# Polysketch attention followed by hashed experts: an early token class of two batches, groups of 256 and 320 slots, and the last weights loaded beside attention

## The chip, the cores and the metric

The kernel runs on one core of a Trainium2 chip. The time is the device time of one execution in microseconds (us); lower is better. The profile is of one execution of the same program and spans from its first to its last instruction, so its span (203.0 us) is a little shorter than the measured time. PE is the matrix engine, DVE the vector engine, ACT the scalar engine, POOL the general engine and SP the engine that only issues transfers.

## The reference

Two stages are chained. The first is a linear attention: queries and keys of 4 batches, 4 heads, 1088 positions and 32 dimensions are mapped to 64 features, which are the outer product of two sketches of 8 numbers.

```
phi(x) = outer(S1 x, S2 x)                    # 8 x 8 = 64 features
kv = sum_s phi(k)[s] v[s];  z = sum_s phi(k)[s]
attn = (phi(q) kv) / (phi(q) z + 1e-6)        # per batch and head
x = attn as rows: 4 * 1088 = 4352 tokens of 4 * 32 = 128 columns
expert of a token = (token_id * 2654435761) % 8
out = relu(x w1[expert]) w2[expert]           # w1 128 x 1024, w2 1024 x 128
```

Everything is in float32. A token is (batch, position), so the first two batches are tokens 0 to 2175. The expert of a token depends on its id alone and not on the attention, so the routing can be worked out while the attention still runs.

## The kernel before, in words

The kernel is one function with the order of every engine written out by hand: each engine executes its instructions in program order, and an instruction waits for the data or the buffer that it needs. In the text, b is the third batch (index 2) and e the fourth (index 3), the last two.

**Attention.** For each batch, keys are transposed on PE, multiplied with the sketches (L383), copied by ACT, and turned into features by DVE (L411). `kv_products` (L442) accumulates kv and z. `kv_diagonal` (L465) spreads the result into a block-diagonal matrix m, and `kv_tail` does so for the last 64 positions. `q_features` makes the query features and transposes them in blocks (fT, L495). `x_products` (L547) multiplies fT with m and ACT copies the product to xe; `x_tail_products` (L557) does the tail. These products use the two PSUM buffers of the pool `ps_x` in turn. `denominators` (L570, L571) and `x_main` (L576) divide, into the single buffer `xs`, and SP stores the rows to the DRAM tensor `x_rows` (L584); `x_tail` (L590, L592) stores the tail. Batch b's rows are stored in two halves, one for each group of query blocks.

**Routing.** Tokens of an expert are counted and ranked on DVE and PE while the first batches run. Each expert has two classes of slots, early and late, of `GN` = 288 slots each. A token may take an early slot only if its row belongs to the first `EP` partitions of the token table; EP covers the first two batches and the first half of the third (2686 tokens). `route_end` writes the tables `get` (row to gather for each slot) and `put` (row to scatter to). There are 16 groups: early slots of experts 0 to 7, then late slots of experts 0 to 7. Should an expert have more tokens than slots, a loop at the end takes the rest in turns.

**Experts.** Slots are handled in chunks of three tiles of 128 slots (`CT` = 3, 12 chunks, while a group is 2.25 tiles). `fetch_tile` (L674) gathers 128 rows by an indirect DMA that POOL issues; `paced` first copies the indices on DVE (L712), so that the gather's place in time is tied to DVE's work. The chunk becomes columns in one of two ways: `bring` transposes it on PE (L722) and evicts it, or `turn_in` splits it into 16-bit halves on DVE (L729), SP transposes them by DMA (L730) and `join_in` puts them together (L734). Before, chunks 0 to 2 are brought and chunks 3 to 11 are turned in.

Group g has eight slots in time; slot c holds `layer1(g, c)` (L789, two matmul instructions) and `layer2(g-1, c)` (L796). ACT and DVE take turns to evict layer1's product with the relu (L680, L682), from four PSUM buffers. Other work is hung on the slots by `at(g, c, ...)`: gathers, chunks, the transposes of results (`turn_out`, `join_out`, L843 and L851) and the scatters to the output (L799).

**Loads.** SP loads the weights of experts 0 to 3 after the inputs, of 4 and 5 after the rows of batch 0 are stored, and of 6 and 7 behind the rows of batch e (L134, L135; 0.5 MB each).

Of the kernel before, what the change touches and what calls it, by code (L numbers as in the profile page):

```python
# [30 lines left out]
def kernel(  # L31
# [31 lines left out]
    GN = 288  # L63
    EB = B - 2
    EP = (EB * S + SM // 2) // C
    NE = EP * C
    HT = E * GN // P
    ST = 2 * HT
    OT = -(-(N - GN) // P)
    WARM = 10  # L70
    assert E * GN % P == 0 and GN >= P and ST <= P
# [42 lines left out]
    def parts(b, tag="q"):  # L114


        return 2 if b == 0 or b == EB and tag == "q" else 1
# [14 lines left out]
    def load_experts(es):  # L132
        for e in es:
            nc.sync.dma_start(w1[:, e], moe_w1[e])  # L134
            nc.sync.dma_start(w2[:, e], moe_w2[e].rearrange("(c p) d -> p c d", p=P))  # L135
# [155 lines left out]
    def route_ranks(cnt):  # L291
        nc.vector.tensor_scalar(took[:], cnt[:, 2], float(GN), None, op0=OP.min)
        nc.vector.tensor_tensor(left[:], cnt[:, 1], took[:], op=OP.subtract)
        nc.vector.tensor_tensor(seq[:], seq[:], cnt[:, 0].unsqueeze(2).to_broadcast([P, E, C]), op=OP.add)
        nc.vector.tensor_mul(seq[:], seq[:], mask[:])
        nc.vector.tensor_reduce(rank[:], seq[:].rearrange("p e c -> p c e"), axis=AX.X, op=OP.add)

    def route_slots():
        nc.vector.tensor_tensor(both[:], mask[:], took[:].unsqueeze(2).to_broadcast([P, E, C]), op=OP.mult)
        took_t = const.tile([P, C], F32, name="took_t")  # L300
        nc.vector.tensor_reduce(took_t[:], both[:].rearrange("p e c -> p c e"), axis=AX.X, op=OP.add)

        late = const.tile([P, C], F32, name="late")
        nc.vector.memset(late[:], 1.0)
        nc.vector.tensor_scalar(late[0:EP], rank[0:EP], float(GN), None, op0=OP.is_gt)
        nc.vector.tensor_tensor(pos[:], rank[:], took_t[:], op=OP.subtract)
        nc.vector.tensor_mul(pos[:], pos[:], late[:])
        slot = const.tile([P, C], F32, name="slot")
        nc.vector.tensor_scalar(slot[:], took_t[:], -1.0, float(E * GN), op0=OP.mult, op1=OP.add)
        nc.vector.tensor_mul(slot[:], slot[:], late[:])  # L310
        nc.vector.tensor_add(slot[:], slot[:], rank[:])
        nc.vector.scalar_tensor_tensor(slot[:], eid[:], float(GN), slot[:], op0=OP.mult, op1=OP.add)
        over = const.tile([P, C], F32, name="over")
        nc.vector.tensor_scalar(over[:], pos[:], float(GN), float(2 * ST * P), op0=OP.is_gt, op1=OP.mult)
        nc.vector.scalar_tensor_tensor(slot[:], slot[:], -1.0, over[:], op0=OP.add, op1=OP.add)
        slot_i = const.tile([P, C], I32, name="slot_i")
        nc.vector.tensor_copy(slot_i[:], slot[:])
        st_i = const.tile([P, 2, C], I32, name="st_i")
        nc.vector.tensor_scalar(st_i[:, 0], slot_i[:], P.bit_length() - 1, None, op0=OP.logical_shift_right)
        nc.vector.tensor_scalar(st_i[:, 1], slot_i[:], P - 1, None, op0=OP.bitwise_and)  # L320
        nc.vector.tensor_copy(st[:].rearrange("p k c x -> p (k c) x"),
                              st_i[:].rearrange("p k c -> p (k c)").unsqueeze(2).to_broadcast([P, 2 * C, 2]))
# [364 lines left out]
    BG, BT = 4, 4 * GN // P  # L687
    assert BG * GN == BT * P and ST % BT == 0
    xTs = {}

    def x_columns(lo, hi):
        b = lo // (BT * P)
        if b not in xTs:
            xTs[b] = rows_in.tile([P, BT * P], F32, tag="xT", name="xT", bufs=2)
        return xTs[b][:, lo - b * BT * P:hi - b * BT * P]
# [3 lines left out]
    CT = 3  # L699
    xg3, turned_in = {}, {}  # L700

    def fetch_tile(i, at_once=False):
        k, j = divmod(i, CT)
        if j == 0:
            xg3[k] = rows_in.tile([P, CT, DM], F32, tag="xg3", name="xg3", bufs=3)
        gather(xg3[k][:, j], get[:, i:i + 1] if at_once else paced(get[:, i:i + 1]), NE if i < HT else N)

    def paced(idx):


        t = moe.tile([P, 1], I32, tag="idx", name="idx", bufs=4)
        nc.vector.tensor_copy(t[:], idx)  # L712
        return t[:]

    def fetch(k):
        for j in range(CT):
            fetch_tile(k * CT + j, True)

    def bring(k):
        xp = ps_x.tile([P, CT, P], F32, tag="x", name="xp")  # L720
        for j in range(CT):
            nc.tensor.transpose(xp[:, j], xg3[k][:, j], ident[:])  # L722
        evict(k, x_columns(k * CT * P, (k + 1) * CT * P), xp[:].rearrange("p a b -> p (a b)"))

    def turn_in(k):
        xh = moe.tile([P, 2, CT * DM], U16, tag="xh", name="xh", bufs=2)
        turned_in[k] = moe.tile([P, 2, CT, P], U16, tag="xh_turned", name="xh_turned", bufs=2)
        for x in range(2):
            nc.vector.tensor_copy(xh[:, x], _half(xg3[k][:].rearrange("p a b -> p (a b)"), x))  # L729
        nc.sync.dma_start_transpose(turned_in[k][:].rearrange("p x a b -> p (x a) b"), xh[:].rearrange("p x b -> p (x b)"))  # L730

    def join_in(k):
        for x in range(2):
            nc.vector.tensor_copy(_half(x_columns(k * CT * P, (k + 1) * CT * P), x),  # L734
                                  turned_in[k][:, x].rearrange("p a b -> p (a b)"))
# [12 lines left out]
    route_end(idx)  # L748
    kp = k_features(abk, T, work, "")
    x_products(b, 0, fTs[0], m)  # L750
    denominators(b, 0, HQ)
    x_main(b, 0, nc.vector)
    fetch(0)
    kv = kv_products(e, (kp, va), (kp_tail, va_tail))
    fT = q_features(abq, 0)
    last_m = kv_diagonal(e, kv)
# [3 lines left out]
    fetch(1)  # L760
    fTs = [fT, q_features(abq, 1)]
    denominators(b, HQ, GQ * HQ + H)
    x_main(b, 1, nc.vector)
    x_tail(b, nc.vector)
    for g in range(GQ):
        x_products(e, g, fTs[g], last_m)
    bring(0)
    x_tail_products(e, m_tail)
# [4 lines left out]
    load_experts(range(E - 2, E))  # L773
# [8 lines left out]
    G = 2 * E  # L782
    hTs, ops = {}, {}

    def layer1(g, c, lo=0, hi=GN):
        if c == 0 and lo == 0:
            hTs[g] = moe.tile([P, FC, GN], F32, tag="hT", name="hT", bufs=2)
        hp = bank([P, GN], "hp")
        nc.tensor.matmul(hp[:, 0:hi - lo], w1[:, g % E, c * P:(c + 1) * P], x_columns(g * GN + lo, g * GN + hi),  # L789
                         start=True, stop=True)  # L790
        evict(c, hTs[g][:, c, lo:hi], hp[:, 0:hi - lo], relu=True)

    def layer2(g, c, lo=0, hi=GN):
        if c == 0:
            ops[g] = ps_o.tile([P, GN], F32, tag="o", name="op")
# [18 lines left out]
    TURN = (G - 3) * GN // P  # L814
# [4 lines left out]
    def half_columns(x, lo, hi):  # L819
        b = lo // (BT * P)  # L820
        if (b, x) not in halves:
            halves[b, x] = moe.tile([P, BT * P], U16, tag=f"half{x}", name=f"half{x}", bufs=2)
        return halves[b, x][:, lo - b * BT * P:hi - b * BT * P]

    def out_columns(g, lo=0, hi=GN):

        mid = min(max(LATE - g * GN, lo), hi)
        if mid > lo:
            for x in range(2):
                nc.scalar.copy(half_columns(x, g * GN + lo, g * GN + mid), _half(ops[g][:, 0:mid - lo], x))  # L830
        if hi > mid:
            nc.scalar.copy(late_cols[:, g * GN + mid - LATE:g * GN + hi - LATE], ops[g][:, mid - lo:hi - lo])
# [41 lines left out]
    def overflow_tables():  # L874
        nc.vector.tensor_scalar(nt[:], left[:], float(P - 1 - GN), 0.0, op0=OP.add, op1=OP.max)
# [19 lines left out]
        nc.vector.tensor_scalar(begin[:], begin[:], float(P), float(GN), op0=OP.mult, op1=OP.add)  # L895
# [11 lines left out]
    at(1, 6, bring, 2)  # L907
    for j, n in enumerate((1, 4, 7)):
        at(*slot(n), fetch_tile, 2 * CT + j)
    for k in range(3, ST // CT):  # L910
        for j in range(CT):
            at(*slot((k * CT * P // GN - 1) * FC - 19 + 7 * j // 2), fetch_tile, k * CT + j)
    for k in range(3, ST // CT):
        first = k * CT * P // GN
        at(first - 1, 0, turn_in, k)
        at(first - 1, 5, join_in, k)
    for g in range(2, G - 1):
        at(g, 1, turn_out, (g - 1) * GN // P)
        at(g, 5, join_out)
        for c in (6, 7):  # L920
            at(g, c, scatter_next)
        at(g + 1, 3, scatter_next)
        if g in (G - 5, G - 2):

# [16 lines left out]

    g, lo = G - 1, GN - P
    mid = g * GN // P
    for c in range(FC):
        layer2(g - 1, c)
        if c == 2:
            scatter_next()
            out_rows(TURN, 2)
# [3 lines left out]
    for c in range(FC):  # L952
        layer1(g, c, 0, lo)
        if c == 3:
            out_rows(TURN + 2, mid - TURN - 2)
# [5 lines left out]
    for c in range(FC):  # L961
        layer1(g, c, lo, GN)
# [4 lines left out]
    assert not ready and mid == TURN + 4 == ST - 3  # L967
    op = ps_o.tile([P, DM], F32, tag="o", name="op_rows")
    for c in range(FC):
        nc.tensor.matmul(op[:], hTs[g][:, c, lo:GN], w2[:, g % E, c], start=(c == 0), stop=(c == FC - 1))  # L970
# [11 lines left out]
    with tc.For_i(0, turns):  # L982
# [37 lines left out]
        xg = rows_in.tile([P, CT, DM], F32, tag="xg3", name="xg3", bufs=3)  # L1020
# [52 lines left out]
```

## Time and profile before

| | |
|---|---|
| time, median of 3 | 204.04 us (203.92 to 204.78) |
| span of the profile | 203.0 us |
| PE busy | 191.7 us (94%) |
| DVE, ACT, POOL busy | 109.1, 75.0, 93.8 us |
| layer1 and layer2 of full width (128x288) | 480 matmul instructions, 78.5 and 76.7 us |
| gathers, scatters | 36 and 36, about 1.0 us each on POOL |
| transposes by DMA in and out | 9 and 26 |
| moved by DMA | 25.82 MB |

Matmuls overlap, so their mean length (414 ns for 128x288) is longer than the distance between two of them; for what PE costs, the distance counts. The line named in a wait is that of the instruction which was the last to signal by the profile, and a wait for several signals can be put down to a wrong one. A label such as 128x288 gives partitions and elements of a partition.

### The profile page before, as it was taken

The numbers are of one execution on the slowest core, as the hardware profiler recorded it, in microseconds if no ns is written. First come the engines' busy times: TensorE is split into PE (matmuls) and PEld (weight loads), VectorE is DVE, ScalarE is ACT, GpSimd is POOL, SyncE is SP. The second block draws the span as 40 slices with busy tenths as digits, with TensorE's granted clock in tenths as the row PEclk, the third lists the DMA queues.
The fourth block names the chain that finished last, engine by engine and source line by source line (L and its number), as shares of the span: only waits on it lengthen the run. The fifth ranks groups of instructions, "written<-read, shape, count | busy, mean of one in ns | idle before, by whom it ended". The sixth has DMA issues, their size and how long they took to land. (4 is left out here: it accounts for less than half of the span.)

```text
span 203.0 us, 3360 instructions
## 1 busy us (share of the span) xinstructions
PE 191.7 (94%) x1081; PEld 158.7 (78%) x1081; DVE 109.1 (54%) x290; ACT 75.0 (37%) x228; POOL 93.8 (46%) x113
## 2 busy tenths in 40 slices
PE   8999999999997899899999999999999999999970
PEld 3798999999996576677777777777777777777970
DVE  6699799999785232242542533633435654331330
ACT  6624965746454222322313223223322323311330
POOL 6002202728018875447427687426677503324750
PEclk9999999999999699999999999999999999999997
DMA  5948999998013179214215224124224133110000
GB/s 140 293 105 244 335 358 347 330 374 268 3 55 95 42 253 332 58 26 120 71 34 129 55 65 103 46 71 110 71 61 99 49 78 85 33 50 26 30 35 12
DMA packets 40321, 25.82 MB, mean 127 GB/s; under 512 B 20730, under 2 KB 37371, under 8 KB 40304
## 3 DMA queue, kind: packets, MB, share of 16 engines
q1 hardware_dynamic: 37840, 20.98, 36.3%
q0 software_dynamic: 2304, 4.59, 7.5%
q8 instruction: 9, 0.15, 0.3%
q14 instruction: 8, 0.07, 0.1%
q10 hardware_dynamic: 160, 0.04, 0.1%
HBM read 17.47 MB, written 4.59 MB: 109 GB/s over the span
## 5 line engine op out<-in xcount | busy, mean ns | idle before, releaser
L789 PE MATMUL hp<-xT,w 128*128 128x288 f32 (+2 forms) x272 | 83.2, 400 | 0.2 <-ACT xT L680 0.2
L796 PE MATMUL op<-hT,w 128*128 128x288 f32 (+1 forms) x256 | 79.1, 399 | 0.0
L682 DVE TENSOR_SCALAR hT<-hp 128x288 f32<-128x288 f32 (+2 forms) x68 | 29.9, 439 | 66.3 <-PE hp L789 55.7
L789 PEld LDWEIGHTS hp<-xT,w 128*128 128x128 f32 x272 | 50.8, 194 | 13.4 <-ACT xT L680 0.3
L796 PEld LDWEIGHTS op<-hT,w 128*128 128x128 f32 x256 | 47.7, 190 | 12.5
L680 ACT ACTIVATE hT<-hp 128x288 f32<-128x288 f32 (+2 forms) x68 | 27.3, 401 | 68.9 <-PE hp L789 68.9
L799 POOL DMA_INDIRECT out_dram<-os,put x36 | 36.4, 1010 | 33.3 <-DVE os L851 14.4
L674 POOL DMA_INDIRECT xg<-x_rows,idx x30 | 31.2, 1040 | 26.0 <-DVE idx L712 19.5
L547 PE MATMUL x_ps<-m,fT 128*128 128x132 f32 x128 | 16.3, 281 | 0.5 <-DVE den L570 0.3
L442 PE MATMUL kv<-va,kp 128*128 128x132 f32 x128 | 15.8, 278 | 0.5 <-ACT va L608 0.5
L547 PEld LDWEIGHTS x_ps<-m,fT 128*128 128x128 f32 x128 | 15.0, 190 | 1.2 <-issue 0.5
L442 PEld LDWEIGHTS kv<-va,kp 128*128 128x128 f32 x128 | 14.9, 190 | 1.0 <-issue 1.0
L576 POOL TENSOR_TENSOR xs<-xe,den 128x512 f32<-128x512 f32 x6 | 7.7, 1300 | 17.2 <-DVE den L571 17.2
L830 ACT COPY half<-op 128x288 uint16<-128x288 uint16 (+1 forms) x26 | 9.1, 400 | 13.0 <-PE op L796 13.0
L674 POOL DMA_INDIRECT xg<-x_rows,get x6 | 7.2, 1200 | 11.7 <-DVE m L465 10.1
L465 ACT COPY m<-kv 32x66 f32<-32x66 f32 x48 | 9.9, 207 | 4.2 <-PE kv L442 3.6
L411 DVE TENSOR_TENSOR f<-ab 128x1024 f32<-128x1024 f32 x8 | 10.6, 1321 | 0.4 <-ACT ab L399 0.2
L495 DVE STREAM_TRANSPOSE fT<-f 128x1024 f32<-128x1024 f32 x8 | 10.0, 1245 | 0.5
L411 DVE TENSOR_TENSOR kp<-ab 128x1024 f32<-128x1024 f32 x8 | 9.4, 1206 | 1.0 <-ACT ab L399 1.0
L383 PE MATMUL ab_ps<-s_k,kT 128*128 128x128 f32 (+3 forms) x72 | 8.9, 276 | 0.2 <-ACT kT L376 0.2
L383 PEld LDWEIGHTS ab_ps<-s_k,kT 128*128 128x128 f32 (+1 forms) x72 | 8.4, 191 | 0.8 <-ACT kT L376 0.4
L550 ACT COPY xe<-x_ps 128x264 f32<-128x264 f32 x16 | 6.0, 380 | 5.5 <-PE x_ps L547 5.2
(157 smaller groups left out, 153.5 us busy)
## 6 DMA issues: line engine op xcount, KB each, us to landing
w<-in_moe_w_dram SPq DMA_DIRECT2D x16, 512.0 KB, 7.5
k<-in_k_dram SPq DMA_DIRECT2D x3, 512.0 KB
v<-in_v_dram SPq DMA_DIRECT2D x3, 512.0 KB, 6.5
q<-in_q_dram SPq DMA_DIRECT2D x4, 256.0 KB, 6.3
q<-in_q_dram SPq DMA_DIRECT2D x2, 512.0 KB, 5.9
x_rows<-xs SPq DMA_DIRECT2D x4, 256.0 KB, 7.5
x_rows<-xs SPq DMA_DIRECT2D x2, 512.0 KB, 4.4
out_dram<-os,put POOLq DMA_INDIRECT x36, 2.3
```

What stands on the lines that cost most here:

```text
L383: nc.tensor.matmul(dst, stationary, s.rearrange("p t x r -> p t (x r)").unsqueeze(1).to_broadcast([s.shape[0], n, s.shape[1], 2 * R]), sta ...
L411: eng.tensor_tensor(dst, ab[:, :, 0].unsqueeze(3).to_broadcast(shape), ab[:, :, 1].unsqueeze(2).to_broadcast(shape), op=OP.mult)
L442: nc.tensor.matmul(kv[:].rearrange("p x y -> p (x y)")[:, pr * HA:(pr + 1) * HA], kp[rows, t, 2 * pr:2 * pr + 2].rearrange("p h i j -> p ( ...
L465: copy(m[f][t * D:(t + 1) * D, h::2, t], src)
L495: nc.vector.transpose(fT[:].rearrange("p k (q s) -> p k q s", q=Q), f[:].rearrange("p q h (k d) -> p (h k) q d", d=D))
L547: nc.tensor.matmul(p[:, h], fT[:, (h0 + h) * FB + fb], m[fb][:, h0 + h].rearrange("p t d -> p (t d)"), start=(fb == 0), stop=(fb == FB - 1 ...
L674: nc.gpsimd.indirect_dma_start(out=dst, out_offset=None, in_=x_dram[0:rows], in_offset=bass.IndirectOffsetOnAxis(ap=idx, axis=0), bounds_c ...
L680: nc.scalar.activation(dst, src, AF.Relu if relu else AF.Copy)
L682: return nc.vector.tensor_scalar(dst, src, 0.0, None, op0=OP.max).ins
L789: nc.tensor.matmul(hp[:, 0:hi - lo], w1[:, g % E, c * P:(c + 1) * P], x_columns(g * GN + lo, g * GN + hi), start=True, stop=True)
L796: nc.tensor.matmul(ops[g][:, 0:hi - lo], w2[:, g % E, c], hTs[g][:, c, lo:hi], start=(c == 0), stop=(c == FC - 1))
L799: st_ = nc.gpsimd.indirect_dma_start(out=out[:], out_offset=bass.IndirectOffsetOnAxis(ap=idx, axis=0), in_=src, in_offset=None, bounds_che ...
```

## The change

The early class now is exactly the first two batches (2176 tokens), so that its gathers need no row of batch b. Its groups have 256 slots, which is two whole tiles, and the late groups have 320; the total stays 4608 slots in 36 tiles. Chunks follow groups, so there are 16 of two or three tiles. The gathers of the first three chunks are issued between the steps of the attention instead of after batch b's rows. Only chunks 0 and 1 are brought through PE; chunks 2 to 15 are turned in. The weights of the last two experts are issued from ACT's queue during the attention of the last two batches instead of from SP behind it. Batch b's rows are divided later, all at once, and stored by one transfer. The divisions of the tables and the tail of the last group are adapted.

```diff
-    EP = (EB * S + SM // 2) // C
+    EP = EB * S // C
...
+    GE, GL = 256, 320
...
-        return 2 if b == 0 or b == EB and tag == "q" else 1
+        return 2 if b == 0 else 1
...
-            xg3[k] = rows_in.tile([P, CT, DM], F32, tag="xg3", name="xg3", bufs=3)
+            xg3[k] = rows_in.tile([P, CT, DM], F32, tag="xg3", name="xg3", bufs=4)
...
     route_end(idx)
+    for j in range(tiles_of(0)[1]):
+        fetch_tile(0, j, True)
     kp = k_features(abk, T, work, "")
+    fetch_tile(1, 0)
     x_products(b, 0, fTs[0], m)
-    denominators(b, 0, HQ)
-    x_main(b, 0, nc.vector)
-    fetch(0)
+    load_experts([E - 2], nc.scalar)
     kv = kv_products(e, (kp, va), (kp_tail, va_tail))
     fT = q_features(abq, 0)
+    fetch_tile(1, 1)
     last_m = kv_diagonal(e, kv)
     x_products(b, 1, fTs[1], m, bank)
     x_tail_products(b, m_tail, bank)
     m_tail = kv_tail(e, kv)
-    fetch(1)
+    load_experts([E - 1], nc.scalar)
     fTs = [fT, q_features(abq, 1)]
-    denominators(b, HQ, GQ * HQ + H)
-    x_main(b, 1, nc.vector)
+    fetch_tile(2, 0)
+    denominators(b, 0, GQ * HQ + H)
+    for g in range(GQ):
+        x_main(b, g, nc.vector)
     x_tail(b, nc.vector)
-    for g in range(GQ):
-        x_products(e, g, fTs[g], last_m)
+    fetch_tile(2, 1)
+    x_products(e, 0, fTs[0], last_m)
     bring(0)
+    x_products(e, 1, fTs[1], last_m)
     x_tail_products(e, m_tail)
     denominators(e, 0, GQ * HQ + H)
     for g in range(GQ):
         x_main(e, g, nc.gpsimd)
     x_tail(e, nc.gpsimd)
-    load_experts(range(E - 2, E))
...
     at(0, 3, bring, 1)
-    at(1, 6, bring, 2)
...
+    for k in range(3, G):
+        for j, c in zip(range(tiles_of(k)[1]), (1, 4, 6)):
+            at(k - 3, c, fetch_tile, k, j)
+    for k in range(2, G):
+        at(k - 1, 0, turn_in, k)
+        at(k - 1, 5, join_in, k)
     for g in range(2, G - 1):
-        at(g, 1, turn_out, (g - 1) * GN // P)
+        at(g, 1, turn_out, first_of(g - 1) // P)
         at(g, 5, join_out)
-        for c in (6, 7):
-            at(g, c, scatter_next)
-        at(g + 1, 3, scatter_next)
-        if g in (G - 5, G - 2):
+        at(g, 6, scatter_next)
+        for c in (0, 2):
+            at(g + 1, c, scatter_next)
+        if g in (G - 4, G - 2):
```

## The prediction

> **What bounds the kernel now.** First the page's slices of the span, which say which engine is full and when:
>
> ```profile
> PE   8999999999997899899999999999999999999970
> PEclk9999999999999699999999999999999999999997
> DMA  5948999998013179214215224124224133110000
> GB/s 140 293 105 244 335 358 347 330 374 268 3 55 95 42 253 332 58 26 120 71 34 129 55 65 103 46 71 110 71 61 99 49 78 85 33 50 26 30 35 12
> ```
>
> A slice is 5.08 us. PE is full almost everywhere, so only what removes PE time or PE gaps pays. The dents are at slices 12, 13 and 15 (61 to 71 and 76 to 82 us), with a clock of 6 tenths in slice 13. DMA is nearly empty in slices 10 to 13, then full in 14 and 15. The busy time by stretch (PE, weight loads, DVE, ACT, POOL; then clock, DMA share, GB/s) narrows that:
>
> ```profile
> 50.00:55.00 5.00, 5.00 (x47) 5.00 (x47) 3.57 (x9) 3.00 (x12) 0.01 (x1) 1.00 0.05 16
> 65.00:67.50 2.50, 1.03 (x6) 0.59 (x6) 0.00 (x0) 0.65 (x2) 1.91 (x2) 0.99 0.39 117
> 67.50:70.00 2.50, 2.40 (x5) 1.83 (x6) 0.65 (x3) 0.72 (x3) 2.17 (x4) 0.50 0.19 52
> 75.00:77.50 2.50, 2.50 (x12) 1.98 (x11) 0.90 (x3) 0.41 (x1) 1.89 (x3) 1.00 1.10 332
> 80.00:82.50 2.50, 1.28 (x7) 0.84 (x7) 0.64 (x3) 0.63 (x2) 1.28 (x2) 1.00 0.68 174
> 100.00:188.00 88.00, 88.00 (x365) 68.95 (x364) 38.51 (x129) 24.20 (x65) 45.29 (x45) 1.00 0.27 70
> ```
>
> From 100 to 188 us nothing is to be won: PE 88.00 of 88. Then the order of time on PE around the dents (start, length, instruction, wait before it):
>
> ```profile
> 62.75 2.04 PE L547 MATMUL x_ps<-m,fT 128*128 128x132 f32 x16 [0.34 <-DVE den L570]
> 64.62 0.27 PE L722 MATMUL xp<-ident,xg 128*128 128x128 f32 x1
> 65.27 0.33 PE L722 MATMUL xp<-ident,xg 128*128 128x128 f32 x1 [0.38 <-DMA xg<-x_rows,get]
> 66.69 0.33 PE L722 MATMUL xp<-ident,xg 128*128 128x128 f32 x1 [1.09 <-DMA xg<-x_rows,get]
> 66.95 0.45 PE L557 MATMUL x_ps<-m_tail,fT_tail 128*64 128x66 f32 x4
> 67.60 3.82 PE L789 MATMUL hp<-xT,w 128*128 128x288 f32 x8 [0.20 <-ACT xT L680]
> 71.58 2.59 PE L789 MATMUL hp<-xT,w 128*128 128x288 f32 x10
> ...
> 80.31 0.38 PE L722 MATMUL xp<-ident,xg 128*128 128x128 f32 x2
> 81.91 0.33 PE L722 MATMUL xp<-ident,xg 128*128 128x128 f32 x1 [1.22 <-DMA xg<-x_rows,idx]
> 82.08 0.65 PE L789 MATMUL hp<-xT,w 128*128 128x288 f32 x2
> ```
>
> Three losses are to be seen. The first group's transposes (L722) wait for their gathers. The eight matmuls after that stand 3.82/8 = 0.478 us apart, against 0.2425 later (74.01 to 74.98 holds four). And at 80 us the third chunk waits for its gather. Why the gathers are late is in the waits of all engines:
>
> ```profile
> POOL xg L674 <- DVE m L465: 10.1, 1, 10.1
> DVE idx L712 <- DMA xg<-x_rows,idx: 5.4, 3, 2.4
> ```
>
> POOL stands idle for 10.1 us with the slot table ready. The DVE named did not release it: the gather begins at 60.16, 4.6 us after the first store of batch 2 (55.59), and such stores land in 4.4 us or more; it reads batch 2's rows. The second wait is DVE held by gathers that share the DMA with the last four weight loads (71.97 to 74.2; 332 GB/s).
>
> **What the Trainium skill says.** "TensorE: Matmul & The Clock Gate", Part 1: an idle activity window of about 3.4 us halves PE's clock, a busy one restores it. The trace agrees in kind: 1.03 busy of 2.5 us, then clock 0.50 for some 3.5 us. "DMA: Bandwidth & Descriptors", "Issuing engines are not separate DMA queues": issuing from another engine saves sequencer time only. So the ACT queue adds no bandwidth; what helps is the hour. Same page, "Anatomy of one DMA": about 2 us of a transfer is fixed, mostly the write receipt. Here 256 KB issued at 63.73 stop moving by about 66 us, and no row shows the receipt itself. "GPSIMD Engine Reference", section 1: POOL shares SBUF interfaces with DVE. The first gather took 2.20 us beside DVE's feature product and 1.00 otherwise, which fits.
>
> **The change, part by part.**
>
> *Group widths.* Per group 32 matmuls. Pitch: 0.2425 us at 288 columns; 0.1153 at 132 (32 between 53.63 and 57.32). The line between them gives 0.2164 at 256 and 0.2686 at 320. 8 x 32 x (0.2164 + 0.2686) = 124.2 us; 16 x 32 x 0.2425 = 124.2. Nothing. The reference's token ids leave at most 310 late tokens for an expert (320 slots), so the overflow loop stays empty, as before.
>
> *First gathers.* They need batches 0 and 1 only; batch 1's rows, issued at 47.39 and 48.73, have landed by about 52, the table is written at 50.7. Four gathers can then run at 52 to 58, where POOL is idle, and bring(0)'s wait disappears.
>
> *Weights through ACT.* Two loads cost SP 1.18 us (71.97 to 73.15). The first pair falls into ACT's wait at 54.3 to 58.1: free. The second pair stands at 61.6, where ACT's next work, the copies of x_products(e,0) at 61.63 and 62.44, frees the two ps_x buffers. They slip to 62.8 to 63.5. PE ends x_products(e,0) at 62.37; bring(0) takes the first buffer at 63.15, x_products(e,1) the second at 63.55, and runs 2.04 to 65.6; the tail products take 0.45, so layer1(0) starts near 66.05 instead of 67.60: gain 1.55. Bounds: issue free on ACT, 65.25 (gain 2.35); issue slow as SP's 3.31 us at 28.34, when its queue was full, 68.2 (loss 0.6). I take 1.18 because the ACT queue is empty then.
>
> *The clock.* PE's longest gap becomes about 0.8 us, so no halving: 71.58 - (67.60 + 8 x 0.2425 + 0.32) = 1.72 us gained. 0.32 is three transposes at 0.107 (two between 185.39 and 185.60).
>
> *Chunks 1 and 2.* bring(1) has two transposes for three: 0.1. bring(2) goes: between 80.31 and 82.08, 1.77 us. Its replacement is turn_in/join_in on DVE and SP. One more transpose in the tail's out_rows: -0.1.
>
> *New wait.* x_main(e) on POOL writes the one xs buffer, which batch 2's store reads. That store is now one 512 KB transfer after both products: DVE ends fT at 62.61, then denominators 0.6, products 2 x 0.69, so issue near 64.8; plus 4.4 (the 512 KB row of the issues) is 69.2. x_main(e) then ends near 71.3 (2.06, row at 68.91). Queued behind it: on SP, batch 3's store, its tail (0.40 POOL + 0.45 issue), then chunk 2's turn_in at about 72.5, landing 2.9 later (median of the nine) at 75.4, or 76.5 beside the store's traffic; join_in 0.6 more: 76.0 to 77.1. PE wants chunk 2 after 66.05 + 3.45 (layer1 of group 0) + 0.2 + 6.9 (group 1) = 76.6. So 0 to 0.5 us of stall; I take 0.3. Also behind x_main(e) on POOL: chunk 3's gathers, landed near 77, just when its turn_in is due; DVE may wait half a microsecond there, covered by four hp buffers. Lower bound 0; upper, if the store lands in 7.5 us (256 KB row's median under load), 3 us.
>
> *Later groups.* Shorter early groups cut the five slots between turn_out and join_out, or turn_in and join_in, by 12%: 4.85 to 4.3 us. The transposes at 108.47 and about 109.7 plus 2.4 land at 112.1, and join_out starts at 112.83: 0.7 spare becomes about 0.1. A DVE wait of some tenths is hidden by the 1.4 us that DVE idles before each eviction. POOL: two gathers and two scatters of 1.3 per 6.9 us group, 75%, as before. Nothing.
>
> Sum: 1.55 + 1.72 + 1.77 + 0.1 - 0.1 - 0.3 = 4.7; 204.04 - 4.7 = **199.3**.
>
> **Rivals.**
> 1. *ACT issues cost nothing on the path and chunk 2 comes in time*: + 0.8 + 0.3, **198.2**. For it: x_products(e,1) waits for DVE's fT till 62.7 anyway. Against: the copies follow the loads directly on ACT. 16%.
> 2. *The stall moves to group 2*: the xs store lands late, SP holds turn_in(2) behind batch 3's store, PE waits 2 to 3 us and keeps the rest: **201.8**. For it: the store shares the DMA with 1 MB of weights, and landings under load took 7.5 us. Against: those weights are nearly through by 66 us at 340 GB/s. 18%.
> 3. *Slower*: the issue on ACT is slow (loss 0.6 instead of gain 1.55, -2.15), PE waits 3 us for chunk 2 and loses its clock again (1.72 back), and later joins miss by 0.1 us in each of 13 groups: 199.3 + 2.15 + 2.7 + 1.72 + 1.3 = **207.2**; without all of it at once about 205. For it: three chains meet on xs, SP and POOL. Against: each has a bound, and four hp buffers stand between. 10%.
>
> **How the numbers follow.** The forecast has 56%, the rivals 16, 18 and 10. The predicted time is the forecast's, 199.3. The range goes from just under rival 1, 197.8, through rival 2 with its wait near the upper bound, 202.4; outside it are rival 3 and some of the edges, under 20%. Over 0.5% faster is below 203.0: the forecast and rivals 1 and 2 save a few hundredths, 0.86. Within 0.5%, 0.05. Slower, 0.09.
>
> **What would show it.** Right: no wait of L722's successor on gathers; PEclk without a 6; layer1's first matmul near 66 us at half its former pitch; DMA busy at 54 to 58 and 62 to 67, quiet at 75 to 79; PE flat from there. Of the terms: the start of bring(0) against ACT's copies gives the issue cost; the start of x_main(e) gives the store's landing; a PE wait on chunk 2's first layer1 gives the new stall. Wrong: ACT's two loads last over 2 us; POOL starts x_main(e) after 71; a second clock dip near 77; PE gaps at each group's start.

## The result, and the profile after

The changed kernel takes **197.93 us** (median of 4 runs, 197.89 to 198.77), the kernel before 204.41 beside it (203.92 to 204.80): a ratio of 0.969, interval 0.966 to 0.973. That is 6.5 us less by the medians (5.5 to 7.0 by the interval). The forecast was 4.7 less, 199.3; the result lies within the forecast's range, but only 0.13 us above its lower end of 197.8, and nearer to rival 1 (198.2) than to the forecast.

The slices of the page after, to be laid beside those of before (a slice is now 4.91 us):

```profile
PE   8999999999999999999999999999999999999980
PEclk9999999999999999999999999999999999999996
DMA  4958999998096552243234324223141422300000
```

The dents in PE are gone, and so is the 6 in the clock. The weights, which filled the DMA in slices 14 and 15 (71 to 81 us), now lie in slices 11 to 13 (54 to 69 us), together with batch 2's store. The order of time on PE, in the columns of before:

```profile
57.26 2.07 PE L547 MATMUL x_ps<-m,fT 128*128 128x132 f32 x16
...
61.53 0.38 PE L737 MATMUL xp<-ident,xg 128*128 128x128 f32 x2
62.17 2.07 PE L547 MATMUL x_ps<-m,fT 128*128 128x132 f32 x16 [0.25 <-ACT xe L550]
64.16 0.45 PE L557 MATMUL x_ps<-m_tail,fT_tail 128*64 128x66 f32 x4
64.54 1.99 PE L809 MATMUL hp<-xT,w 128*128 128x256 f32 x8
66.37 0.38 PE L737 MATMUL xp<-ident,xg 128*128 128x128 f32 x2
66.59 2.32 PE L809 MATMUL hp<-xT,w 128*128 128x256 f32 x10
```

No transpose waits for a gather. Eight matmuls of layer1 (now L809) and two transposes take 2.05 us (64.54 to 66.59), where eight matmuls and three transposes took 3.98. One wait of 0.25 is left.

Where did the time come from? The two traces are best laid over each other at an event ahead of all edits that matter: the x_products of group 1 of batch b, at 57.96 us before and 57.26 after. Below it is called the mark. Those 0.70 us arise in the first 6 us of the program, which the change doesn't touch, and the changed kernel scatters by as much: in another trace of it (z0_after) the mark lies at 58.08. From the mark on:

| from the mark | before | after | gained |
|---|---|---|---|
| to layer1's first matmul | 9.64 | 7.28 | 2.36 |
| layer1's first half of group 0, with the transposes behind it | 3.98 | 2.05 | 1.93 |
| third chunk on PE, with its wait (80.31 to 82.08) | 1.77 | 0 | 1.77 |
| to the start of the last scatter | 139.35 | 133.62 | 5.73 |

The parts add to 6.06; 0.21 of the second is the narrower group, given back by the wide ones, and a transpose more in the tail takes 0.11: 5.74 against the 5.73 measured. Nothing was lost in the other 120 us. Two more traces of the changed kernel or a variant that takes the same time (z0_after, y4_loads_sp) have 133.62 as well. The span behind the last scatter is 0.4 shorter; it differs by 0.3 between two traces of the changed kernel too.

### The profile page after: what moved, and what is told of

Same layout as the page of the kernel before. It is cut to its first block, busy times and chain, and to the rows that moved or that the text cites. A ratio compares the mean times of both kernels' runs of the same rounds, so it can differ in the third digit from the quotient of the medians.

```text
span 196.2 us, 3370 instructions
## 1 busy us (share of the span) xinstructions
PE 188.3 (96%) x1077; PEld 157.6 (80%) x1077; DVE 112.9 (58%) x313; ACT 74.2 (38%) x227; POOL 93.6 (48%) x113
## 5 line engine op out<-in xcount | busy, mean ns | idle before, releaser
L809 PE MATMUL hp<-xT,w 128*128 128x256 f32 (+3 forms) x272 | 81.5, 392 | 0.0
L817 PE MATMUL op<-hT,w 128*128 128x256 f32 (+2 forms) x256 | 79.0, 399 | 0.0
L682 DVE TENSOR_SCALAR hT<-hp 128x256 f32<-128x256 f32 (+3 forms) x68 | 29.9, 440 | 62.9 <-PE hp L809 50.9
L809 PEld LDWEIGHTS hp<-xT,w 128*128 128x128 f32 x272 | 50.1, 190 | 11.4
L680 ACT ACTIVATE hT<-hp 128x256 f32<-128x256 f32 (+3 forms) x68 | 27.2, 400 | 66.5 <-PE hp L809 66.5
L674 POOL DMA_INDIRECT xg<-x_rows,idx x34 | 34.8, 1022 | 27.1 <-DVE idx L726 12.4
L852 ACT COPY half<-op 128x256 uint16<-128x256 uint16 (+1 forms) x26 | 8.9, 391 | 13.2 <-PE op L817 13.2
L745 DVE COPY xh<-xg 128x256 uint16<-128x256 uint16 (+1 forms) x28 | 8.7, 352 | 0.0
L751 DVE COPY xT<-xh_turned 128x256 uint16<-128x256 uint16 (+1 forms) x28 | 8.3, 350 | 0.1
```

The lines of the kernel that those rows point to most:

```text
L674: nc.gpsimd.indirect_dma_start(out=dst, out_offset=None, in_=x_dram[0:rows], in_offset=bass.IndirectOffsetOnAxis(ap=idx, axis=0), bounds_c ...
L680: nc.scalar.activation(dst, src, AF.Relu if relu else AF.Copy)
L682: return nc.vector.tensor_scalar(dst, src, 0.0, None, op0=OP.max).ins
L817: nc.tensor.matmul(ops[g][:, 0:hi - lo], w2[:, g % E, c], hTs[g][:, c, lo:hi], start=(c == 0), stop=(c == FC - 1))
```

## The experiments

Theory: two waits were removed, each with its own cause: the first gathers waited for batch 2's rows (and PE's idling halved its clock), the third chunk's gathers ran beside 2 MB of weights. The rivals: the transfers alone are the cause; or the new widths and the chunks that left PE bring the gain. The runs stand in three groups, each on one chip with the kernel before beside it: x1 to x4 (208.3 us for the kernel before), x5 and y0 to y2 (207.9), z0 to z2 and y4 (204.4). In the traces of the two slower chips PE stands still for 0.5 to 1.7 us at some places (in x1_class_only at 125 and 158 us) where the first trace has no gap and where no edit was made. So totals are compared within a group, and places in a trace are counted from the mark. The kernel before has a trace only from the first measurement and none on the slower chips; where a trace of theirs is set against it, that is said of the stretch near the mark alone.

**One cause at a time.** First the class alone:

```diff
-    EP = (EB * S + SM // 2) // C
+    EP = EB * S // C
```

> The kernel before with one line changed: the early class ends at the second batch. Groups, chunks and loads stay. Theory (the first gathers wait for batch 2's rows, and PE's idling halves its clock): the first wait goes and with it the slow matmuls, layer1 starts at about 65.6 us of the span instead of 67.6 (2.0) and the clock keeps full (1.7), while the third chunk's wait of 1.3 near 80 us stays: 204.0 - 3.7 = 200.3. Rival (POOL's gathers are slow in themselves, or the transfers are what counts): under 1 us gained, 203 or more.

Measured: 207.68 against 208.34, ratio 0.997 (0.994 to 1.000): 0.7 us less, at most 1.3, where 3.7 was forecast. The trace on PE says why:

```profile
57.69 2.07 PE L547 MATMUL x_ps<-m,fT 128*128 128x132 f32 x16
...
65.61 2.21 PE L789 MATMUL hp<-xT,w 128*128 128x288 f32 x8
67.66 0.49 PE L722 MATMUL xp<-ident,xg 128*128 128x128 f32 x3
67.98 2.59 PE L789 MATMUL hp<-xT,w 128*128 128x288 f32 x10
...
77.01 0.27 PE L722 MATMUL xp<-ident,xg 128*128 128x128 f32 x1
77.79 0.33 PE L722 MATMUL xp<-ident,xg 128*128 128x128 f32 x1 [0.50 <-DMA xg<-x_rows,idx]
79.69 0.33 PE L722 MATMUL xp<-ident,xg 128*128 128x128 f32 x1 [1.57 <-DMA xg<-x_rows,idx]
...
81.05 1.16 PE L789 MATMUL hp<-xT,w 128*128 128x288 f32 x2
```

The first half of the mechanism was as foretold. POOL's first gather begins at 52.10 us instead of 60.16, so it was batch 2's rows that it had waited for. Layer1 starts at 65.6 and its first eight matmuls run at full pitch: 10.29 us from the mark to layer1's second half against 13.62, 3.3 gained. But counted from the mark PE comes 3.0 us earlier to the third chunk (19.32 against 22.35), while its last tile comes only 1.95 earlier (22.00 against 23.95); x3 below shows that it is the weights which hold those gathers. The wait grew from 1.2 to 2.1 us, and behind it the clock is halved: a pair at 1.16 instead of 0.65. Six pairs later (84.46, before 84.99) the lead is 26.77 against 27.03 from the mark: of 3.3 us, 0.3 is left. What the first wait gave, the second took; without the halved clock behind it, 1.95 would have been left.

Then the loads alone (the same two calls on ACT's queue as in the change, put behind fetch(0) and fetch(1) of the kernel before):

```diff
     fetch(0)
+    load_experts([E - 2], nc.scalar)
...
     fetch(1)
+    load_experts([E - 1], nc.scalar)
...
-    load_experts(range(E - 2, E))
```

> The kernel before with only the last two experts' weights moved to ACT's queue during the attention. Theory: the third chunk's wait near 80 us goes (1.3), the first wait and the clock dip stay: 202.7, or 203.2 if the second pair of loads delays the first gathers. Rival (the loads merely move the contention onto the first gathers): 204 to 206.

Measured: 207.79, ratio 1.001 (0.997 to 1.0045): no difference that can be told from the scatter. On PE:

```profile
66.48 0.30 PE L722 MATMUL xp<-ident,xg 128*128 128x128 f32 x1 [1.55 <-DMA xg<-x_rows,get]
67.74 0.68 PE L722 MATMUL xp<-ident,xg 128*128 128x128 f32 x2 [0.96 <-DMA xg<-x_rows,get]
...
69.00 2.21 PE L790 MATMUL hp<-xT,w 128*128 128x288 f32 x8 [0.20 <-issue]
...
80.61 0.49 PE L722 MATMUL xp<-ident,xg 128*128 128x128 f32 x3
```

The third chunk's wait is gone, as the theory has it. But batch 2's store and the first gathers now share the DMA with the weights: POOL's first gather begins at 62.23 us instead of 60.16, and PE's waits for these gathers are 2.8 us in all (0.28 of it at chunk 1) against 1.5: layer1 starts 10.89 us after the mark (58.11 here), 1.25 later than before. That is the rival's effect, and these two about cancel. The theory was wrong on the clock: it had the dip stay, and here the eight matmuls take 2.21 us, full speed, behind a longer wait. This puts the trace 0.9 us ahead of before's by the matmul at 84.22 (before 84.99); the totals of the group don't show that much.

Both together:

> The kernel before with the early class of two batches and the loads on ACT together, groups still 288 and chunks of three tiles. Theory (the two causes add): 204.0 - 3.7 - 1.3 = 199.0, and the rest to the changed kernel (1.1) belongs to the chunks that left PE and to the order of bring(0). Rival (the group sizes are what makes it work): 200.5 or more.

Measured: **203.00**, ratio 0.977 (0.969 to 0.984), 5.3 us less. From the mark layer1 starts after 8.00 us, and the third chunk waits 0.33. The theory's forecast of 5.0 holds; that the two causes add does not. Alone they give 0.7 and 0.5 by the medians, together 5.3. About 1 us of that is not theirs for certain: the two gaps at places without an edit are 1.7 us in all in this trace and 2.7 in those of x1 and x2. The rest is still more than three times the sum of the two. Early gathers meet late weights, early weights meet late gathers; only with both early does PE wait for neither. The rival on the group sizes falls: they are 288 here, and chunks have three tiles. What the full change brings beyond this (it is 7.2 us below the kernel before in the next group) was not taken apart by runs; its traces reach layer1 0.72 us sooner after the mark (7.28) and have no transposes of a third chunk on PE.

**The clock.** Idle matmuls on constant data fill PE's wait; the wait itself stays.

```diff
             nc.tensor.transpose(xp[:, j], xg3[k][:, j], ident[:])
+            if k == 0:
+                keep_busy((2, 5, 0)[j])
```

> The kernel before with seven idle matmuls on constant data put between the first chunk's transposes, where PE waits anyway: the wait stays, only PE's idleness goes. Theory (idleness costs the clock): layer1's first eight matmuls stand 0.24 us apart instead of 0.48, 1.7 us gained: 202.3. Rival (the clock falls for another reason at that time): no gain, 204 to 204.5.

Measured: 209.06, ratio 1.006 (1.003 to 1.009), 0.7 us slower, and layer1's matmuls still 0.48 apart. It does not tell the theories apart: in its trace ACT stood still for 2.5 us before the eviction (named "remote"), so PE idled for 2.1 us behind the tail products instead. So four more were put there:

> The kernel before with idle matmuls between the first chunk's transposes and four more behind the tail products, so that PE hardly idles before layer1 though the wait stays. Theory (idleness costs the clock): layer1's first eight matmuls 0.24 us apart, 1 to 1.7 us gained. Rival: they stay 0.48 apart, no gain.

Measured: 209.39 against 207.91, ratio 1.007 (1.004 to 1.009), 1.5 us slower where 1 to 1.7 of gain was forecast. On PE:

```profile
67.18 1.04 PE L187 MATMUL idle<-warm 128*128 128x512 bf16 x4
68.06 2.10 PE L792 MATMUL hp<-xT,w 128*128 128x288 f32 x8
...
82.40 0.33 PE L722 MATMUL xp<-ident,xg 128*128 128x128 f32 x1 [1.40 <-DMA xg<-x_rows,idx]
```

Eight matmuls in 2.1 us: kept busy, PE keeps its clock, although it comes to them 10.18 us after this trace's mark (57.88), later than before's 9.64. The time did not fall, because what was won is again waited off at the third chunk (2.1 us here).

That fits the theory but does not prove it: one trace shows one execution, and PE has kept its clock behind waits too. All traces together show this. In this stage the clock fell in four of them, each time for one stretch of 3.4 us behind a wait of PE: of 1.5 us in two pieces (before), of 2.1 (x1 and x4), of 5.9 (y1 below). It fell in none in which PE had no wait of 1 us here (x3, the changed kernel, y4, z1, z2). But x2 waited for 2.8 us, y2 below for 2.5 in one piece and x5 for 2.1 at the third chunk, and all three kept it. So the clock fell only behind waits, and not behind all of them; what decides is not shown. None of the waits but y1's was as long as the 3.4 us for which the clock then stayed down.

Single executions differ accordingly. The changed kernel had a mean granted clock (the share of full speed that PE was allowed) of 0.990 or more in all 12 of its executions. The kernel before had 0.984 to 0.996 in the 75 that the three comparisons rest on, and the 35 of them under 0.99 took 0.6 to 0.9 us longer than the others of their group, by the medians. That agrees with a dip which about half of the executions have; only the traced ones show where it lies.

**The loads in the changed kernel.** The base on this chip:

> The changed kernel itself, as the base for its variants on the same chip: 0.97 of the kernel before, 6 us less.

Measured: 200.69, ratio 0.964 (0.959 to 0.970), 7.2 us less. Now the loads back where they were:

```diff
-    load_experts([E - 2], nc.scalar)
...
-    load_experts([E - 1], nc.scalar)
...
     x_tail(e, nc.gpsimd)
+    load_experts(range(E - 2, E))
```

> The changed kernel with the last two experts' weights issued from SP behind batch 3's rows, as before the change. Theory (the hour of the loads counts, because SP's queue and the DMA are then in front of the second chunk's transposes): chunk 2's transposes go out 2 us later and land 2 to 3 us later, PE waits 1 to 3 us before group 2 and again for later chunks: 2 to 4 us slower than the changed kernel. Rival (four PSUM buffers and the chunks' lead hide it): under 0.5 us slower.

Measured: 208.48, ratio 1.004 (1.0015 to 1.006): 7.8 us slower than the changed kernel, slower even than the kernel before. The direction was right, but 2 to 4 us were forecast. What SP issues (start, length), then what DVE and PE wait for:

```profile
70.73 0.58 SPq L134 DMA_DIRECT2D w<-in_moe_w_dram  x1
...
72.48 0.43 SPq L135 DMA_DIRECT2D w<-in_moe_w_dram  x1
73.09 10.79 SPq L746 DMA_TRANSPOSE xh_turned<-xh  x2
```

```profile
81.43 0.52 DVE L751 COPY xT<-xh_turned 128x256 uint16<-128x256 uint16 x2 [6.93 <-DMA xh_turned<-xh]
```

```profile
82.05 1.19 PE L808 MATMUL hp<-xT,w 128*128 128x256 f32 x2 [5.86 <-issue]
```

The four issues hold SP for 2.2 us (70.73 to 72.91), as forecast. But the transposes of chunk 2 then took until 81.4, 8.3 us, behind 2 MB of weights; in the first trace of the changed kernel 3.0 at most. DVE stood in its join for 6.9 us with evictions behind it, PE for 5.9, and the clock was halved after that. These two make up most of the loss, so it lies at this place, and not in the gaps that differ between chips. Is it chunk 2's transposes alone, or the loads' hour in general? With chunk 2 through PE, on a third chip:

```diff
+    at(1, 6, bring, 2)
-    for k in range(2, G):
+    for k in range(3, G):
         at(k - 1, 0, turn_in, k)
```

> The changed kernel again, as the base on this chip: 0.965 to 0.97 of the kernel before.

> The changed kernel with chunk 2 brought through PE in slot (1,6) instead of turned by DMA. Theory (the 1.77 us at chunk 2 before were nearly all a wait for the gather, and the gather is now early): two transposes more and no wait, 0.2 to 0.4 us slower than the changed kernel. Rival (turning it off PE is what saved them): 1 us or more slower.

> Loads back on SP behind batch 3's rows, as in y1_loads_back, but chunk 2 through PE, so that it doesn't stand behind the loads. If y1's loss came only from chunk 2's transposes behind the loads on SP: within 1.5 us of the changed kernel. If the loads hold chunk 3 as well (gathers and transposes beside 2 MB of weights): chunk 3 is waited for next, 2 to 5 us slower than the changed kernel.

Measured: the changed kernel 198.55, ratio 0.971 (0.965 to 0.976); chunk 2 through PE 198.80, 0.973 (0.968 to 0.979); that and the loads back 199.30, 0.974 (0.969 to 0.979). Differences this small drown in the scatter of the totals, and the traces decide: from the mark to the last scatter z1 takes 133.85 us, the changed kernel 133.62. So two transposes more cost about 0.23, and of chunk 2's old 1.77 us all but some 0.3 were a wait and not work. The late loads cost 0.5 us more by the medians and 1.1 in the trace (134.94), once nothing that is due at once goes through SP behind them. On DVE of the last, then on PE:

```profile
78.39 0.50 DVE L745 COPY xh<-xg 128x256 uint16<-128x256 uint16 x2 [2.28 <-DMA xg<-x_rows,idx]
...
83.24 0.51 DVE L751 COPY xT<-xh_turned 128x256 uint16<-128x256 uint16 x2 [1.94 <-DMA xh_turned<-xh]
```

```profile
83.85 0.67 PE L808 MATMUL hp<-xT,w 128*128 128x256 f32 x2 [0.86 <-ACT half L851]
```

Chunk 3 is late by 2.3 and 1.9 us, but a group's lead and four PSUM buffers leave 0.9 of it on PE. In x1_class_only the late loads hurt more, although chunk 2 went through PE there too: its gathers were issued beside the loads, here before them.

**ACT's issues.** The disputed term of the prediction, doubled twice:

```diff
-    load_experts([E - 1], nc.scalar)
+    for i in range(0, FC, 2):
+        nc.scalar.dma_start(w1[:, E - 1, i * P:(i + 2) * P], moe_w1[E - 1][:, i * P:(i + 2) * P])
+        nc.scalar.dma_start(w2[:, E - 1, i:i + 2], moe_w2[E - 1].rearrange("(c p) d -> p c d", p=P)[:, i:i + 2])
```

> The changed kernel with the last expert's two loads cut into eight on ACT's queue, so that ACT issues four times as often there. Theory of the prediction (issue time on ACT holds up ACT's copies behind it): 6 more issues of 0.4 us, the copies of the last query products 2 us later, PE waits for their buffers, 1.5 to 2 us slower than the changed kernel. Rival (ACT issues while its copies of earlier work still run, so the time is hidden): slower only by what exceeds the 1 us of work ACT has queued, about 1 us, or nothing.

Measured (same group as y0_after): 202.94, ratio 0.9765 (0.970 to 0.983), 2.25 us slower than the changed kernel, a little over the theory's 1.5 to 2. ACT, issues (ACTq) and copies, then PE:

```profile
60.69 0.35 ACTq L779 DMA_DIRECT2D w<-in_moe_w_dram  x1
60.85 0.39 ACT L550 COPY xe<-x_ps 128x264 f32<-128x264 f32 x1
61.08 0.45 ACTq L780 DMA_DIRECT2D w<-in_moe_w_dram  x1
...
61.29 0.44 ACT L473 COPY m_tail<-kv 64x66 f32<-64x66 f32 x2
...
64.09 0.45 ACTq L780 DMA_DIRECT2D w<-in_moe_w_dram  x1
64.63 0.66 ACT L550 COPY xe<-x_ps 128x264 f32<-128x264 f32 x2 [2.90 <-DMA w<-in_moe_w_dram]
```

```profile
65.06 0.44 PE L737 MATMUL xp<-ident,xg 128*128 128x128 f32 x2 [2.54 <-ACT xe L550]
```

The first two issues run while ACT is still copying what was queued ahead of them. They end at 61.53, the copies at 61.73: free. The six more stand alone, and the copy behind them starts at 64.63; PE waited 2.5 us for it. So the mechanism of the prediction exists, and so does the rival's: issues hold up a copy only as far as they outlast the work queued ahead of them.

Last, the early loads from SP at the same places:

> The changed kernel with the early loads issued from SP at the same two places instead of from ACT. Theory (the hour counts and not the engine, and SP has nothing else to do then): within 0.3 us of the changed kernel. Rival (SP's issue time delays batch 2's store and all that follows): 0.5 to 1.5 us slower.

Measured: 198.21, ratio 0.971 (0.966 to 0.976), the same as the changed kernel. SP, having nothing to wait for, issued the loads from 48.5 to 50.7 us, 4 to 10 us earlier than ACT does. Neither the engine nor these microseconds count here; before batch 3's rows or behind them does. None of the variants beats the changed kernel by more than its scatter.

## Why the prediction was right

*Group widths* (0): right; the pieces of the table close to 0.01 us without a term for them.

*First gathers* and *Weights through ACT* (1.55): the mechanism was right, the gain is 2.36, the prediction's bound for issues that are free (2.35). The mis-sized term is the 0.8 us that ACT's second pair of issues should have cost PE: it cost nothing, since 0.80 us of issues (0.35 and 0.45, not the 1.18 taken from SP) fit beside the copies queued ahead. This was rival 1's case. The prediction counted issue time as if ACT did one thing at a time.

*The clock* (1.72): 1.6 between the two traces (1.93 in the table less 0.21 for the narrower group and 0.11 for a transpose less), and in every trace with a fall PE had just waited. But the prediction read it from one trace, of an execution of 204.7 us, and took every execution to be like it. By the granted clocks about half of them have no dip, so over executions the term is worth at most half of that, as an estimate. That the trace which was read had a dip was chance, and it made the term look certain.

*Chunks 1 and 2* (1.77 and 0.1): right; z1_bring2 shows that nearly all of it was a wait.

*New wait* (0.3): 0. Batch 2's store of 512 KB landed in less than was taken:

```profile
x_rows<-xs SPq DMA_DIRECT2D x3, 512.0 KB, 3.4
```

3.4 us in the median of three such stores, instead of 4.4. On POOL x_main(e) began 3.6 after the store's issue (63.86), and chunk 2's transposes went out at 70.75:

```profile
67.44 2.05 POOL L576 TENSOR_TENSOR xs<-xe,den 128x512 f32<-128x512 f32 x2 [2.08 <-DVE idx L726]
```

DVE's join, 73.75 to 74.33, found them landed, and PE's first layer1 on chunk 2 stands at 75.23. So rival 2's chain was real, with about 0.9 us to spare, and y1_loads_back shows what happens when it is longer.

*Later groups* (0): right. DVE waited three times for a transpose, 1.6 us in all, and PE not once.

Taken together, the terms erred by 1.0 us: 0.8 for ACT's issues and 0.3 for the new wait, less 0.1 for the clock. The rest of the distance between 4.7 and 6.5 belongs to no term of the prediction: in the two traces it lies in the start and the end of the program, where executions scatter. So the mechanism was right and the sum too small, and that its range still held the result is owed to the lower end, which rival 1 had set.

What the prediction did not say is that its two main terms depend on each other. It priced them as a sum, and in the change both were made, so the sum came out; either one alone was forecast at 1.3 to 3.7 us of gain before its run and brought almost none.

## What to carry to other kernels

When the bound engine waits at two places in a row, removing the first wait alone only brings it earlier to the second: ask of each saved microsecond which later arrival is set by something else than the engine, as a transfer behind other transfers is. Bulk loads belong where the DMA is idle, and what matters is which short, urgent transfers they stand in front of, less which engine issues them. Transfer issues on ACT were free here as long as the work queued ahead of them lasted. And a stretch at half clock in one trace need not be in every execution: look at several before it is counted as a gain.

## What the runs showed of the hardware

- ACT's transfer issues (0.35 and 0.45 us for 512 KB each) ran beside its own earlier copies; eight of 128 KB in a row (3.8 us) left ACT without work for 2.9 us before its next copy (y2_loads_split).
- The clock fell for 3.4 us at a time, behind waits of PE of 1.5 to 5.9 us, and stayed full behind others of 2.1 to 2.8.
- The DMA transposes of a chunk (two of 128x256 16-bit halves) landed within 3.0 us of their first issue in the changed kernel, and after 8.3 behind 2 MB of loads (y1_loads_back).
- The first gather took 2.20 us before and 2.05 after, both times beside DVE's feature products, but 1.23 in x2_loads_only, where DVE was transposing. Later gathers issued beside these products were long too (1.42 and 1.82 us in x1_class_only). That fits what the Trainium skill ("GPSIMD Engine Reference", section 1) says of two-input DVE work and the shared interfaces. But not all such work does it: the gather at 62.67 us before took 1.00 beside DVE's division, which also has two inputs.
- The kernel before took 204 us in the first measurement and in one group, and 208 in the two groups on other chips. The traces from these have PE gaps of 0.5 to 1.7 us for which the profile names no cause or different ones. What they are stays open.
